# New gates, a split first weight load and a new instruction order in a fused sparse-attention and gated feed-forward kernel

## The chip, the core and the metric

The kernel runs on one core of a Trainium2 chip. Such a core has four engines that compute, each with its own queue of instructions: TensorE (PE in the profile; loading its weights is the row PEld), VectorE (DVE), ScalarE (ACT) and GpSimd (POOL). SyncE (SP) computes nothing here and issues loads and stores; GpSimd issues loads as well. Sixteen DMA engines carry the transfers. The metric is the device time of one execution in microseconds (us). The kernel before took 286.05, 288.70 and 288.79 us in three runs, median 288.7.

## The reference

Two parts follow each other. The first is causal attention in which each query sees only six chunks of 32 keys, chosen by an upper bound on its scores:

```python
B, H, S, D = 4, 8, 768, 64;  chunk, top_k = 32, 6;  nc = S // chunk
k_min, k_max = min and max over each chunk of k
ub = sum(maximum(q * k_min, q * k_max), axis=-1)          # one bound per query and chunk
ub = where(causal by chunk, ub, -1e9);  top_chunks = argsort(ub)[..., -6:]
scores = q @ k.T / sqrt(D);  masked to the chosen chunks and to pos_q >= pos_k
attn = softmax(scores) @ v
```

The second is a gated feed-forward layer over the 4 x 768 = 3072 tokens with 512 columns and 1536 hidden columns: `(sigmoid(x @ w_gate) * (x @ w_val)) @ w_out`. All inputs and the output are float32.

## The kernel before

**Units.** The work is cut into rows of 128 queries, six to each of the four batches, and these into units of up to three. Unit u0 holds the first row of batches 0, 1 and 2; u1 holds rows 1 to 3 of batch 0; u2 holds rows 4 and 5 of batch 0 and the first row of batch 3; u3 to u7 hold the rest in order. For each unit the kernel prepares keys and queries (`prepare`), chooses chunks (`choose`), computes scores, exponents and values (`attend`), and puts the result through the feed-forward layer (`ffn`; `ffn_pair` for u4 with u5 and u6 with u7, in a form with fewer products).

**The first rows.** A first row sees only its own four chunks, so there is nothing to choose, and `first` handles it by itself. The suffix _b is the batch. The loads are kf0_b and kf1_b (keys of even and odd heads), qf0_b and qf1_b (queries), vf_b (values). kfT_b and qfT_b are four float32 turns each on TensorE; kf16_b and qf16_b cast the results; scf_b are the scores, expf_b_0 and _1 the exponents on ScalarE, cmf_b_0 and _1 the causal mask on GpSimd, pvf_b the products with the values, rzf_b and xf_b the division on VectorE, xpsf_b and xTf_b turn the result into xT of the unit. All three batches have to be through before g_u0_0, the first gate product of the feed-forward layer.

**Unit 1 and 2.** Their raw keys and queries come by pairs of heads: k0_u1 to k3_u1, q0_u1 to q3_u1, and the same for u2, each load 192 KB for u1 and 128 KB for u2. `turned` copies each piece (kn_, qn_), turns it on TensorE (kT_, qT_), and copies it out in several forms (kt_, kx0_, kx1_, hk0_, hk1_ for keys; qf_, qm_, hq0_, hq1_ for queries). ub_u1 computes the bounds, ubn and ubm copy them with the causal limit, mx and ap find the chosen chunks, apt and hqm bring the choice into the rows that are added to the scores.

**Other work of the head.** hkp with three digits is the pattern of the chunks, copied from `epat` into the key tiles, eight copies of 64 x 1536 elements. beat0, beat1 and so on are turns of the identity matrix on TensorE whose results nobody reads; `BEATS` holds how many each consists of. v_b_i loads 128 rows of values and v16_b_i casts them; v16_0_0 casts vf_0.

**Weights.** wg0 to wg2 and wv0 to wv2 load 512 hidden columns each of the gate and value weights, wo0 to wo2 the output weights. They are issued on GpSimd's queue and convert to 16 bits on the way. So that they don't compete with the first loads, they read the results of gates: after0 to after6 copy one element of a landed load into the tile `word`. In the kernel before the gates stand on the four query loads of u1 and on vf_0, vf_1 and vf_2. Products g_u_i and v_u_i (four matmuls each) need wg(i // 4) and wv(i // 4).

**The order.** Each of these steps is an `Op` of a `Plan`. The text `ORDER` lists all of them once, and each engine runs its own in that order, strictly. A word is name@engine:slots: the engine is given where the step can run on several and it is not the first choice, and the slots say which buffer of a kind its result takes (eight PSUM banks, six landing buffers "v" of 128 rows, two "osb", two "big" for raw keys and queries, seven "np", and so on). A step that takes a slot waits until its last user is done; a load that reuses a landing buffer therefore holds up SyncE's queue, and all loads and stores behind it, until the cast or turn that reads the buffer has run.

## Time and profile before

| | us |
|---|---|
| runs | 286.05, 288.70, 288.79 |
| median | 288.70 |
| profiled execution, its own time | 288.5 |
| span of that execution, first instruction to last | 286.6 |
| granted TensorE clock | 1.00 of full speed |
| TensorE busy with instructions of line 953 (g and v of u0 to u3) | 39.0 and 39.1 |
| TensorE busy with line 984 (the output products of u0 to u3) | 35.2 |
| ScalarE busy with line 875 (184 exponents) | 89.1 |

The rows that follow further down come from one profiled execution. A row of the timeline reads: start in us, duration in us, engine, line of the kernel, operation, output<-input, partitions x elements and type, count, and in brackets the idle time before it with what ended it. A group row ends in: busy time, mean in ns of one, idle time before, and its releaser. A row of waits reads: engine, tile and line that waited, what it waited for, total us, number of waits and the longest. A row of the table by stretches reads: stretch, its length, then busy us (and instructions) of PE, PEld, DVE, ACT and POOL, the mean granted clock, the mean busy share of the DMA engines and GB/s. A row of a DMA issue reads: output<-input, queue, operation, count, KB of each, and us from issue to landing. SPq and POOLq are the queues of SyncE and GpSimd, where an issue's duration is the time that the queue spent at it. Unit and batch numbers are left out of the names by the profile.

### The profile page before, as it was taken

The page shows a single profiled execution, that of the slowest core. Times are in us where ns is not written, and L with a number is a line of the kernel's source. Part 1 is how long each engine was busy: PE and PEld are TensorE (multiplying, and loading weights), DVE is VectorE, ACT ScalarE, POOL GpSimd, SP SyncE. Part 2 cuts the span into 40 slices and gives each one's busy share as a digit, 9 for nine tenths or more (in the row PEclk, how much of TensorE's full clock was granted, in tenths as well). Part 3 has the DMA queues.
Part 4 walks back from the last instruction along what each step waited for, and adds up shares of the span by engine and source line. Part 5 has one row for each costly group of instructions (what it writes and reads, how often), then busy time and mean ns, then how long its engine had stood idle before and what let it go on. Part 6 is the DMA issues. An engine that isn't in the chain of part 4 may idle for free.

```text
span 286.6 us, 7418 instructions
## 1 busy us (share of the span) xinstructions
PE 269.3 (94%) x2735; PEld 185.0 (65%) x2735; DVE 243.2 (85%) x663; ACT 210.5 (73%) x458; POOL 158.2 (55%) x232
## 2 busy tenths in 40 slices
...
DMA  6999999999999968929708415202000102010005
GB/s 181 271 244 178 202 196 198 185 170 217 168 214 155 232 141 164 167 71 207 130 1 173 93 31 134 93 2 45 14 17 0 30 16 106 5 75 37 3 0 220
DMA packets 130035, 34.28 MB, mean 120 GB/s; under 512 B 118096, under 2 KB 127056, under 8 KB 130000
## 3 DMA queue, kind: packets, MB, share of 16 engines
...
q14 instruction: 14, 0.11, 0.1%
...
## 4 chain that ended last, share of the span: by engine, by line
PE 70%; DMA 10%; DVE 7%; SPq 4%; ACT 3%; POOL 2%; issue 2%; ACTq 0%; DVEq 0%; POOLq 0%
PE sc_u L864 10%; PE o_u L984 10%; PE v_u L953 8%; PE g_u L953 8%; PE pv_u L897 5%; DMA wv<-in_moe_w_val_dram 5%; PE suo_u6u L1211 3%; PE ube_u L802 2%; DMA q<-in_q_dram 2%; PE sug_u6u L1070 2%; PE suo_u4u L1211 2%; PE suv_u6u L1070 2%; PE sug_u4u L1070 2%; SPq L553 2%; PE suv_u4u L1070 2%
## 5 line engine op out<-in xcount | busy, mean ns | idle before, releaser
L875 ACT ACTIVATE att_u<-sc_u 128x512 f16<-128x512 f32 (+3 forms) x184 | 89.1, 555 | 11.6 <-PE sc_u L864 11.0
L881 POOL TENSOR_SCALAR_AFFINE_SELECT att_u<-att_u 128x384 f16<-128x384 f16 (+1 forms) x56 | 31.4, 567 | 37.6 <-ACT att_u L875 35.6
L953 PE MATMUL g_u<-xT_u,wg 128*128 128x384 f16 x192 | 39.0, 326 | 3.3 <-DVE osb_u L994 2.5
L953 PE MATMUL v_u<-xT_u,wv 128*128 128x384 f16 x192 | 39.1, 326 | 2.8 <-DMA wv<-in_moe_w_val_dram 2.8
L961 ACT ACTIVATE gate_u<-g_u 128x384 f16<-128x384 f32 x48 | 23.6, 494 | 21.2 <-PE g_u L953 19.8
L984 PE MATMUL o_u<-wo,hg_u 128*128 128x512 f16 x144 | 35.2, 379 | 0.0
L965 DVE SCALAR_TENSOR_TENSOR hg_u<-gate_u,v_u 128x384 f16<-128x384 f16 x48 | 24.9, 537 | 5.8 <-PE v_u L953 4.0
L864 PE MATMUL sc_u<-hqe,hke 128*128 128x128 f16 (+2 forms) x220 | 27.8, 243 | 0.4 <-DVE c0g_u4u L1085 0.2
L953 PEld LDWEIGHTS <-wg 128*128 128x128 f16 x192 | 18.4, 98 | 15.0 <-issue 4.2
L897 PEld LDWEIGHTS <-att_u 128*128 128x128 f16 x640 | 24.7, 97 | 5.2 <-issue 1.3
L953 PEld LDWEIGHTS <-wv 128*128 128x128 f16 x192 | 18.1, 98 | 14.4 <-DMA wv<-in_moe_w_val_dram 3.6
L897 PE MATMUL pv_u<-v,att_u 128*128 128x65 f16 x640 | 26.8, 193 | 0.0
L864 PE MATMUL sc_u<-hqo,hko 128*128 128x128 f16 (+2 forms) x220 | 25.3, 243 | 0.5 <-DVE c1v_u4u L1085 0.5
L579 POOL CAST v<-v 128x512 f16<-128x512 f32 x23 | 15.2, 668 | 13.6 <-DMA v<-in_v_dram 13.3
L864 PEld LDWEIGHTS <-hke 128*128 128x128 f16 x220 | 16.8, 98 | 7.1 <-issue 1.2
L984 PEld LDWEIGHTS <-hg_u 128*128 128x128 f16 x144 | 13.3, 98 | 11.7 <-issue 0.2
L864 PEld LDWEIGHTS <-hko 128*128 128x128 f16 x220 | 16.4, 98 | 6.5 <-issue 1.4
L916 DVE TENSOR_TENSOR x_u<-pv_u,rz_u 128x384 f16<-128x384 f32 (+1 forms) x28 | 14.9, 532 | 0.9
L1193 POOL TENSOR_TENSOR v<-hgp_u 128x384 f16<-128x384 f16 x5 | 4.5, 910 | 18.3 <-DVE hgp_u L1100 16.8
L769 DVE STREAM_TRANSPOSE qf_u<-q 128x384 f32<-128x384 f32 (+2 forms) x28 | 11.6, 437 | 3.1 <-DMA q<-in_q_dram 3.1
L825 DVE MAX8 mx_u<-ubn_u 128x8 f32<-128x8 f32 (+16 forms) x152 | 12.7, 159 | 0.1
L587 DVE TRANSPOSE_TENSOR_REDUCE kcr<-k 128x24 f32<-128x768 f32 x12 | 11.3, 957 | 1.5 <-issue 0.8
...
## 6 DMA issues: line engine op xcount, KB each, us to landing
v<-in_v_dram SPq DMA_DIRECT2D x23, 256.0 KB, 4.3
...
out_dram<-osb_u SPq DMA_DIRECT2D x16, 256.0 KB, 2.7
wg<-in_moe_w_gate_dram POOLq DMA_DIRECT2D x3, 512.0 KB, 11.1
wv<-in_moe_w_val_dram POOLq DMA_DIRECT2D x3, 512.0 KB, 11.3
wo<-in_moe_w_out_dram POOLq DMA_DIRECT2D x3, 512.0 KB, 13.1
out_dram<-osb_u6u SPq DMA_DIRECT2D x5, 256.0 KB, 2.0
```

The costliest lines, as they stand in the source:

```text
L579: plan.add(f"v16_{b}_{ib}", {POOL: pool(H * D)}, lambda e: nc.gpsimd.tensor_copy(v16[b % 2][:, ib, :, 0:D], at(t)), reads=[t], writes=[("v ...
L864: nc.tensor.matmul(at(t)[:, o:o + 128 * m], hk[b % 2][e_][:, p, 128 * jb:128 * jb + 128], hq[u.side][e_][:, p, 128 * x:128 * (x + m)], sta ...
L875: plan.add(f"exp_{u.name}_{h}_{y}", {ACT: act(n)}, lambda e, t=t, att=att, b0=b0, n=n: nc.scalar.activation(at(att)[:, b0:b0 + n], at(t), ...
L881: nc.gpsimd.affine_select(out=dv, in_=dv, compare_op=ALU.is_ge, fill=0.0, base=0, pattern=[[0, u.m], [1, 128]], channel_multiplier=-1)
L897: nc.tensor.matmul(at(pv)[:, last, x, :], at(att)[:, c:c + 128], v16[b % 2][:, jb, h, :], start=(jb == 0), stop=(jb == ib))
L916: plan.add(f"x_{u.name}_{p}", {DVE: dve(u.t)}, lambda e: nc.vector.tensor_tensor(at(x_).rearrange("p a (e d) -> p e a d", e=2), at(pv)[:, ...
L953: nc.tensor.matmul(at(t), w16[:, c, 128 * fb:128 * fb + 128], at(u.xt)[:, c, :], start=(c == 0), stop=(c == 3))
L961: plan.add(f"tanh_{u.name}_{fb}", {ACT: act(T)}, lambda e, g=g, gate=gate: nc.scalar.activation(at(gate), at(g), AF.Tanh, scale=0.5), read ...
L965: plan.add(f"hg_{u.name}_{fb}", {DVE: dve(T)}, lambda e, w_=w_, gate=gate, hg=hg: nc.vector.scalar_tensor_tensor(at(hg), at(gate), 1.0, at ...
L984: nc.tensor.matmul(at(o), hgs[c][1][1]()[:, 128 * tb:128 * tb + 128], wo16[:, fc, lo:hi], start=(c == 0), stop=(c == NFB - 1))
L1070: nc.tensor.matmul(at(t), left[i](c), right[i](c), start=first and c == 0, stop=c == 1, skip_group_check=not first)
L1211: nc.tensor.matmul(at(t), sums[what[i][0], f][1]()[:, 128 * tb:128 * tb + 128], what[i][1](f), start=first and f == 0, stop=f == half - 1, ...
```

## The change

Four things are changed. (1) The weights' gates: instead of seven, there are three, on the second halves of the query loads of the first rows (qf1_0, qf1_1, qf1_2). (2) The first weights: wg0 is split. A quarter of its rows, wgp, reads no gate at all; the other three quarters, still called wg0, read the three gates. The gate products of unit 0 wait for both. (3) BEATS: 17 groups with 79 turns in place of 12 groups with 67. (4) ORDER is another text throughout: other positions, engines and slots for the same steps. Counted over the whole text, 28 steps go from GpSimd to VectorE, 26 from GpSimd to ScalarE, 31 from ScalarE to VectorE, 27 from VectorE to ScalarE, 19 from VectorE to GpSimd and 16 from ScalarE to GpSimd. Of the diff of ORDER, the part up to just behind g_u0_0 is shown; behind it the text goes on in the same way to the end. The added lines shift the line numbers of the code by three from `weights` on (953 becomes 956).

```diff
-BEATS = (16, 12, 2, 1, 12, 6, 1, 4, 6, 2, 3, 2)
+BEATS = (17, 11, 3, 4, 4, 7, 6, 2, 5, 1, 2, 2, 4, 3, 1, 2, 5)
 
 ORDER = """
-v10 q0_u1:0 qn_u1_0:0 k3_u1 ident ap1 epat0:0 epat kcr0 hkp001 q2_u2:1 k0_u1 kn_u1_0:1 kn_u1_3@POOL:2 hkp011@POOL
-beat0:7 kT_u1_3:0 kt_u1_3:0 hkp010@ACT qT_u1_0:1 q0_u2 k1_u1 kT_u1_0:2 kt_u1_0@DVE:1 hk1_u1_0@ACT kn_u1_1@POOL:2
-kx1_u1_0:0 kT_u1_1:3 kx1_u1_1 kf0_0:0 kf1_0 kfT_0:4 kt_u1_1:2 kf16_0:2 hkf0@ACT hkf1@ACT qf_u1_0:0 kxf0 kf0_1:1 k2_u1
-kn_u1_2@DVE:1 q3_u1 hk0_u1_0 qn_u1_3:0 kxf1:1 hk0_u1_3@POOL kcr_f after0 qf1_0:2 qf0_0 beat1:7 qfT_0:5 qf16_0@DVE:3
-vf1_1:4 hk0_u1_1@POOL qn_u2_0@POOL:5 beat2:7 qT_u2_0:4 beat3:7 scf_0:5,1,1 expf_0_1:2 kT_u1_2:6 kx0_u1_1 qT_u1_3:3
-qf_u1_3@DVE q2_u1 hk1_u1_1@POOL kf1_1 qf1_1:0 kfT_1:7 after3 q1_u1 qn_u1_1:1 qT_u1_1:1 hq0_u1_3@DVE k3_u2 expf_0_0
-qf_u1_1 k2_u2 hq0 kx0_u1_3 vf_1:0 hq0_u1_1 qn_u1_2@POOL:5 qT_u1_2:3 qf_u1_2 kt_u1_2:2 kx1_u1_3 qm_u1_2@ACT:0
-hkp000@POOL vf1_3:5 hq1_u1_0@POOL qm_u1_1@ACT vf_0:2 qf0_1 kf1_2:1 cmf_0_0 q3_u2 cmf_0_1 beat4:5 qfT_1:3 qf16_1:1
-hq0_u1_0 kx1_u1_2 v16_0_0 beat5:5 pvf_0_0:3 qn_u2_2@POOL:0 qT_u2_2:0 vc_1@ACT ident16 vf1_2:2 after5 kf16_1@DVE:3
-kx0_u1_2 scf_1:6,7,1 expf_1_0 qf_u2_0:1 expf_1_1:3 pvf_0_1:1 vf_2:1 vc_2@ACT kx0_u1_0 qm_u1_0 kcr_u1 qm_u1_3 beat6:5
-ub_u1:2,5 rzf_0_0:0 rzf_0_1:1 xf_0_1:0 kn_u2_2@DVE:1 kT_u2_2:7 k1_u2 q1_u2 after6 after2 kf0_2 kfT_2:4 kf16_2:1
-xf_0_0:1 hk0_u1_2 xpsf_0_1:3,0 ubn0_u1:0 kx1_u2_2:0 ubm0_u1 mx0_u1:0 qf0_2:3 after4 qf1_2 qfT_2:2 qf16_2:3 xpsf_0_0:1
-xTf_0_0@ACT after1 wg0 wv0 beat7:6 scf_2:2,4,2 ubn1_u1 ap0_u1 apt0_u1:0 cmf_1_1 pvf_1_1:1 qf_u2_2 xTf_0_1@ACT cmf_1_0
-pvf_1_0:5 wg1 ubm1_u1 rzf_1_0:0 xf_1_0:1 hq1_u1_3@POOL qn_u2_1@DVE:4 beat8:6 qT_u2_1:5 xpsf_1_0:3 expf_2_0 cmf_2_0
-rzf_1_1:0 kn_u2_1:1 xf_1_1:0 xpsf_1_1:1 expf_2_1:1 kt_u2_2@DVE:1 pvf_2_0:4 rzf_2_0:0 xTf_1_1 xf_2_0:0 cmf_2_1 beat9:6
-pvf_2_1:2 qm_u2_0@POOL:0 qf_u2_1 qn_u2_3:4 hqm0_u1_2@ACT beat10:6 sc_u1_3_0:4,2 xpsf_2_0:1 hqm0_u1_0@DVE sc_u1_1_0:5,3
-sc_u1_1_1:0 xTf_1_0@ACT qm_u2_2@ACT hq0_u1_2@DVE sc_u1_3_1:3 wv1 rzf_2_1:0 xTf_2_0 xf_2_1:0 exp_u1_3_0 kn_u2_3@POOL:2
-kT_u2_3:1 kx0_u2_2 exp_u1_1_0 exp_u1_1_1 v_0_2:0 kf1_3:4 xpsf_2_1:2 xTf_2_1 sc_u1_3_2:4 mx1_u1 hkp110@POOL qT_u2_3:6
-qf_u2_3@DVE ap1_u1 apt1_u1 v11 sc_u1_1_2:5 sc_u1_2_0:7,1 cm_u1_1 exp_u1_3_2 cm_u1_3 v_0_3:5 wg2 kx0_u2_3 kT_u2_1:0
-kx1_u2_1 exp_u1_2_0 cm_u1_2 hkp100 hk1_u2_2 g_u0_0:2,0,0 tanh_u0_0 sc_u1_2_1:6 exp_u1_2_1 hq1_u1_2 beat11:4 v_u0_0:7
-g_u0_1:6,1,1 v_u0_1:2 kx0_u2_1 tanh_u0_1 g_u0_2:4,2,2 hg_u0_1 hg_u0_0 v_u0_2:6 exp_u1_3_1 exp_u1_1_2 hkp111 hkp101
...
+v11 k2_u1:0 epat0:0 ident q1_u2:1 hq0 kcr0 epat k3_u1 q3_u1 q1_u1 qf1_0:0 hkp110 qn_u2_1:0 qf0_0 hkp010@ACT hkp111
+k0_u2 kn_u1_2@POOL:1 ap0 k1_u1 kn_u1_3@POOL:2 beat0:7 kT_u1_2:0 k0_u1 hkp000@ACT kf0_0:1 kf1_0 kt_u1_2@DVE:0 q0_u2
+kx0_u1_2 qn_u1_1:1 hk1_u1_2@POOL qn_u1_3:3 kx1_u1_2:0 kf0_1:2 hkp101@ACT q0_u1 beat1:7 qT_u1_3:0 kn_u2_0@POOL:4
+qfT_0:1 after0 kf1_1 wgp hkp001 kT_u2_0:2 kT_u1_3:3 q2_u1 kn_u1_1@POOL:4 kx0_u1_3 kt_u1_3:1 q2_u2 hkp011@ACT
+kn_u1_0@POOL:2 qf_u1_3@DVE:0 beat2:7 kT_u1_1:4 qf1_2:0 qT_u2_1:5 ap1 v10 kT_u1_0:0 kf0_2:3 qm_u1_3:0 kfT_0:6 kx1_u1_3
+kt_u1_0:2 qf16_0@DVE:2 qn_u2_0:0 kf16_0:4 beat3:7 qT_u2_0:3 kx0_u1_0 qT_u1_1:1 kxf1:1 qf_u1_1 qf0_2 kx0_u1_1 qf_u2_0:1
+beat4:7 scf_0:7,1,1 hq0_u1_3 vf_0:1 hq0_u2_0@POOL hk0_u1_2@ACT hk1_u1_3@POOL qm_u1_1@ACT qn_u1_0@DVE:2 hq1_u1_3@DVE
+expf_0_0 beat5:3 qT_u1_0:3 vf_1:0 kx1_u1_1 expf_0_1:2 cmf_0_0 kx1_u1_0 qn_u1_2:2 kf1_2 qf_u2_1@DVE vf1_2:1 qn_u2_2:0
+kcr_u1@POOL beat6:7 qT_u1_2:0 qf1_1:4 qf_u1_0 cmf_0_1 qT_u2_2:5 qfT_2:1 qf0_1 qm_u1_0@ACT qf_u1_2@DVE vf1_1:2 hq1_u1_1
+kfT_1:3 ident16 k2_u2 kt_u1_1@DVE:0 v16_0_0 q3_u2 kxf0 beat7:7 pvf_0_0:4 qf0_3:1 kf16_1@DVE:0 vc_1@ACT vf_2:1 beat8:7
+kfT_2:3 qf16_2@DVE:3 qf1_3 after1 qm_u1_2@POOL kf16_2:5 kf1_3:3 qfT_1:1 qf_u2_2 beat9:7 scf_2:3,6,1 v_0_3:2 after2
+pvf_0_1:5 qf16_1:6 hq0_u1_1@DVE wv0 rzf_0_0:0 expf_2_1:3 kcr_f hkp100 kf0_3 wg0 beat10:7 ub_u1:1,0 hk1_u1_1@ACT
+hq0_u1_0@DVE k1_u2 vc_2@ACT xf_0_0:0 cmf_2_1 v_0_2:0 rzf_0_1:1 kn_u2_2:3 xf_0_1:1 wg1 pvf_2_1:4 expf_2_0 scf_1:6,7,0
+v_0_1:4 ubn0_u1:0 kT_u2_2:5 hk0_u1_0@ACT hq1_u1_0@POOL ubm0_u1 qfT_3:3 kx1_u2_0:1 expf_1_0 rzf_2_1:1 cmf_2_0 xf_2_1:2
+hkf0@ACT mx0_u1:0 cmf_1_0 beat11:1 xpsf_2_1:4,0 pvf_2_0:6 xpsf_0_0:1 qf16_3:1 rzf_2_0:1 hk0_u1_1 qn_u2_3:3 ap0_u1
+beat12:3 pvf_1_0:3 kt_u2_0:0 ubn1_u1 v16_0_3 expf_1_1:0 rzf_1_0:0 beat13:0 qT_u2_3:0 xf_1_0:0 xTf_0_0@ACT cmf_1_1
+xTf_2_1 hq0_u1_2 beat14:7 xpsf_1_0:3 xf_2_0:2 wv1 apt0_u1:0 xTf_1_0@ACT beat15:7 xpsf_2_0:6 hqm0_u1_0@DVE xTf_2_0@ACT
+hqm0_u1_2 beat16:7 kfT_3:6 pvf_1_1:3 hq0_u2_2@POOL sc_u1_0_0:4,3 kf16_3:3 sc_u1_1_1:1,0 rzf_1_1:1 sc_u1_1_0:7 xf_1_1:2
+k3_u2 exp_u1_0_0 qf_u2_3@DVE xpsf_1_1:3 xpsf_0_1:6 xTf_1_1 sc_u1_2_0:0,2 xTf_0_1@ACT cm_u1_0 kx0_u2_0 sc_u1_2_2:4
+sc_u1_2_1:3 exp_u1_1_0 ubm1_u1 g_u0_0:6,0,0 wg2 kx1_u2_2 exp_u1_2_0 qm_u2_1:0 k10_1:0 qm_u2_2 v_u0_0:7 mx1_u1
+tanh_u0_0 cm_u1_2 hq1_u2_3 g_u0_1:0,1,1 ap1_u1 exp_u1_1_1 cm_u1_1 v_u0_1:6 tanh_u0_1 wv2 hk0_u1_3 hk1_u1_0@ACT
+g_u0_2:1,2,2 hg_u0_1 exp_u1_2_1 wo0 v_u0_2:0 hq1_u1_2@DVE tanh_u0_2 g_u0_3:3,1,3 exp_u1_2_2 hq1_u2_0@POOL hg_u0_2
+qm_u2_3@ACT wo1 kt_u2_2:2 v_u0_3:4 kn_u2_1@DVE:2 tanh_u0_3 hq1 hg_u0_0 hkf1 sc_u1_3_0:0,1 sc_u1_3_1:3 hg_u0_3
...
-    word = lone("word", [1, 7], F32)
+    word = lone("word", [1, 3], F32)
...
     def weights(i, prio, after):
-        lo, hi = 512 * i, 512 * i + 512
-        return plan.add(f"wg{i}", {POOL: (760, 760)}, lambda e: nc.gpsimd.dma_start(wg16[:, :, lo:hi], wgs[:, :, lo:hi]),
+        lo, hi, c0 = 512 * i, 512 * i + 512, int(i == 0)
+        if c0:
+            plan.add("wgp", {POOL: (760, 760)}, lambda e: nc.gpsimd.dma_start(wg16[:, 0:1, lo:hi], wgs[:, 0:1, lo:hi]),
+                     reads=[], writes=[("wg", "p")], prio=-19.0, dma=(3000, 2048))
+        return plan.add(f"wg{i}", {POOL: (760, 760)}, lambda e: nc.gpsimd.dma_start(wg16[:, c0:4, lo:hi], wgs[:, c0:4, lo:hi]),
...
-            op = plan.add(f"g_{u.name}_{fb}", pe(650), product(g, wg16), reads=xt + [("wg", fb // 4)], writes=[g, "ffn"],
+            op = plan.add(f"g_{u.name}_{fb}", pe(650), product(g, wg16), reads=xt + [("wg", fb // 4)] + ([("wg", "p")] if u.i == 0 else []), writes=[g, "ffn"],
...
-    after((units[1].raw, 1, 0), lambda t: t[0:1, 1, 0, 0, 0, 0:1], 0)
-    after((units[1].raw, 1, 1), lambda t: t[0:1, 1, 1, 0, 0, 0:1], 1)
-    after((units[1].raw, 1, 2), lambda t: t[0:1, 1, 2, 0, 0, 0:1], 2)
-    after((units[1].raw, 1, 3), lambda t: t[0:1, 1, 3, 0, 0, 0:1], 3)
-    after(raw_f[0]["v"], lambda t: t[0:1, 0, 0:1], 4)
-    after(raw_f[1]["v"], lambda t: t[0:1, 0, 0:1], 5)
-    after(raw_f[2]["v"], lambda t: t[0:1, 0, 0:1], 6)
-    late = [f"after{i}" for i in range(7)]
+    after((raw_f[0]["q"], 1), lambda t: t[0:1, 1, 0:1], 0)
+    after((raw_f[1]["q"], 1), lambda t: t[0:1, 1, 0:1], 1)
+    after((raw_f[2]["q"], 1), lambda t: t[0:1, 1, 0:1], 2)
+    late = [f"after{i}" for i in range(3)]
```

328 lines of the change are left out of this document (163 added, 165 removed).

## The prediction

> **What bounds the kernel now.** I read the page first, then the waits of TensorE, its busy time in three stretches, the timeline around the first feed-forward products, and last the DMA queues.
>
> ```profile
> span 286.6 us, 7418 instructions
> PE 269.3 (94%) x2735; PEld 185.0 (65%) x2735; DVE 243.2 (85%) x663; ACT 210.5 (73%) x458; POOL 158.2 (55%) x232
> DMA  6999999999999968929708415202000102010005
> ```
>
> TensorE is the bound, and in the first third the DMA engines are full as well. Where TensorE is not busy is told by a table of stretches (first column the stretch in us, then busy times).
>
> ```profile
> 0.00:30.11 30.11, 23.78 (x236) 19.25 (x237) 20.65 (x73) 22.31 (x45) 22.40 (x46) 1.00 0.98 217
> 30.11:282.90 252.79, 245.51 (x2502) 165.74 (x2499) 222.17 (x591) 188.17 (x413) 135.83 (x187) 1.00 0.55 108
> 180.00:227.00 47.00, 46.21 (x488) 31.43 (x486) 45.88 (x97) 45.46 (x105) 30.12 (x38) 1.00 0.10 25
> ```
>
> At 30.11 the first gate product g_u0_0 starts, at 282.90 the last product ends. Between them 252.79 us pass and TensorE is idle for 252.79 - 245.51 = 7.3 us. The 30.11 us before are another world: most of TensorE's work there is small, and 65 of the 67 identity turns are in it. The third row is the one stretch where VectorE (45.88) and ScalarE (45.46) are as full as TensorE (46.21 of 47).
>
> ```profile
> PE v_u L953 <- DMA wv<-in_moe_w_val_dram: 2.8, 3, 1.1
> PE g_u L953 <- DVE osb_u L994: 2.5, 1, 2.5
> 30.11 0.81 PE L953 MATMUL g_u<-xT_u,wg 128*128 128x384 f16 x4
> 32.00 0.82 PE L953 MATMUL v_u<-xT_u,wv 128*128 128x384 f16 x4 [0.64 <-DMA wv<-in_moe_w_val_dram]
> 32.66 0.81 PE L953 MATMUL g_u<-xT_u,wg 128*128 128x384 f16 x4
> 38.84 0.82 PE L953 MATMUL v_u<-xT_u,wv 128*128 128x384 f16 x4 [1.13 <-DMA wv<-in_moe_w_val_dram]
> 45.54 0.82 PE L953 MATMUL v_u<-xT_u,wv 128*128 128x384 f16 x4 [1.06 <-DMA wv<-in_moe_w_val_dram]
> 54.40 0.65 PE L615 MATMUL kfT<-ident,kf 128*128 128x128 f32 x4
> ```
>
> Of the 7.3 us, the value weights cost 0.64 + 1.13 + 1.06 = 2.8: TensorE reaches v_u0_0, v_u0_4 and v_u0_8 before wv0, wv1 and wv2 land. From one such landing to the next but one piece pass 38.84 - 32.00 and 45.54 - 38.84, so a full piece of weights passes every 3.4 us. Product follows product after 32.66 - 32.00 = 0.66 us. The last row, kfT_3, turns the keys of block 3; it stands behind all the gate and value products of unit 0, at 54.40.
>
> **The equation.** If G is the start of g_u0_0 and nothing else changes, span = G + (252.79 - 2.8) + (286.6 - 282.9) = G + 253.7. The new order puts a little more real work ahead of g_u0_0: four-transpose turns qfT_3 and kfT_3 come in, two-transpose turns and about one score group go out. I take 0.6 us (the two turns at 0.65 each, less what leaves), so span = G + 253.1. Before, G was 30.1 with the 2.8 behind it; the new order breaks even at G = 33.5. Everything hangs on G.
>
> **The change part by part.** *Gates and first weights.* The order gives GpSimd wgp behind after0, and the first gated piece is now wv0, behind after1, qm_u1_2 and after2; wg0 follows with three quarters of its bytes.
>
> ```profile
> 14.66 0.45 SPq L542 DMA_DIRECT2D kf<-in_k_dram  x1
> 19.15 0.28 POOL L513 COPY word<-vf 1x1 f32<-1x1 f32 x1 [0.55 <-DMA vf<-in_v_dram]
> 19.84 1.05 POOL L518 DMA_DIRECT2D wg<-in_moe_w_gate_dram  x1
> 20.89 0.76 POOL L519 DMA_DIRECT2D wv<-in_moe_w_val_dram  x1
> 26.66 0.85 POOL L603 TENSOR_SCALAR qm_u<-qf_u 128x256 f32<-128x256 f32 x1
> ```
>
> The load that opens the gate is qf1_1, SyncE's 25th. Before, the 25th was vf_2, and it let `word` go at 19.15. The bytes of the first 25 loads are nearly equal (by their sizes 128 KB fewer), and wgp adds a quarter of a piece, 0.25 x 3.4 = 0.85 us on full DMA engines. So the gate opens at about 19.6. Then qm_u1_2, 320 columns against the 256 of the row, takes about 1.0, and wv0 issues near 20.9, 1.1 us later than wg0 did. wgp's own issue (0.76 to 1.05) delays two copies behind it on GpSimd by as much; ScalarE is not ready for their results by then, so I take nothing, with 1.0 as the bound. wgp's gain is 0.85 us at wg0's landing.
>
> *ScalarE's share of the head.*
>
> ```profile
> 3.37 0.51 ACT L358 COPY qn_u<-kq_u 128x384 f32<-128x384 f32 x1 [1.29 <-DMA kq_u<-in_q_dram]
> 6.64 1.47 ACT L358 COPY hko<-epat 64x1536 f16<-64x1536 f16 x1
> 10.92 0.48 ACT L358 COPY qf_u<-qT_u 128x384 f32<-128x384 f32 x1
> 12.88 0.60 ACT L657 ACTIVATE attf<-scf 128x512 f16<-128x512 f32 x1 [0.94 <-PE scf L652]
> 9.67 0.69 DVE L625 TENSOR_REDUCE kcr<-kfT 128x16 f32<-128x512 f32 x1 [1.07 <-ACT kf L358]
> ```
>
> Four of the eight pattern copies now run on ScalarE instead of one: 4 x 1.47 = 5.9 us, all ahead of the first exponents. With the 15 other instructions up to qn_u1_2 at about 0.5 each (7.4 us), and a start near 3.7 with half a microsecond of waits, qn_u1_2 ends near 17.5. That is late for three things in a row. qT_u1_2 (TensorE) follows at 18.1; vf1_1 waits for its buffer, and v16_0_0 behind it on GpSimd is done near 18.8; SyncE waits for that to reuse v16_0_0's landing slot (qf0_3). On VectorE, qf_u1_2, ident16, kt_u1_1, kxf0 and kf16_1 follow, five instructions of up to 0.69, 2.6 us in all, so kfT_2 cannot turn before 20.7, and kf1_3, which lands where kf_2 lay, issues near 21.3. So the tail of SyncE's head loads (kf1_3, v_0_3, kf0_3) starts just after wv0.
>
> *What the weights do to those loads.* The rows give for single issues the KB and the us to landing; the first is the kf issue of 14.66, then follow those of 19.53, 20.68 and 25.34, whose issue rows stand below them.
>
> ```profile
> kf<-in_k_dram SPq DMA_DIRECT2D x1, 128.0 KB, 2.7
> kf<-in_k_dram SPq DMA_DIRECT2D x1, 128.0 KB, 8.0
> v<-in_v_dram SPq DMA_DIRECT2D x1, 256.0 KB, 13.4
> kf<-in_k_dram SPq DMA_DIRECT2D x1, 128.0 KB, 20.6
> wg<-in_moe_w_gate_dram POOLq DMA_DIRECT2D x1, 512.0 KB, 8.8
> 19.53 1.11 SPq L542 DMA_DIRECT2D kf<-in_k_dram  x1
> 20.68 0.90 SPq L573 DMA_DIRECT2D v<-in_v_dram  x1
> 25.34 6.87 SPq L542 DMA_DIRECT2D kf<-in_k_dram  x1
> ```
>
> Alone, a kf load takes 2.7 us. Once weights flow, kf1_3 landed at 19.53 + 8.0 = 27.5 and v_0_3 at 20.68 + 13.4 = 34.1: 256 KB in 6.6 us, so 128 KB in 3.3. kf0_3 landed at 45.9, and nobody minded, since kfT_3 stood at 54.40 and the casts of v_0_x were late too. In the new order two near consumers hang on them. kfT_3 stands on TensorE ahead of the last scores and of g_u0_0; and v16_0_3 stands on GpSimd ahead of cmf_1_1 and of wv1.
>
> *G with late keys.* If kf1_3 still slips through (21.3 + 2.7 = 24.0), v_0_3 lands at 30.6 and kf0_3 at 33.9. If it doesn't, it lands about 7.7 us behind wv0's issue as before (28.6), v_0_3 at 35.2; but by then wv0 (20.9 + 8.8 = 29.7), wg0 (32.2) and wg1 (35.6) are through and wv1 is held, so kf0_3 comes near 36.3. Bounds 33.9 and 36.3, I take 35.2. From there to g_u0_0: the turn (0.65), its cast and one exponent on ScalarE (0.60 each by the row of 12.88), xpsf_0_1 and xTf_0_1 (under 0.5): 2.3 us. G = 37.5.
>
> wv1 then issues between 33 and 35 and needs at most the 8.8 of a first piece; v_u0_4 stands nine products (5.9) and about 1 us of scores behind G, at 44.4. So no weight wait is left, which is why the 2.8 goes.
>
> *Identity turns.* 79 instead of 67, and all of them now stand ahead of G: 14 more at 0.11 to 0.21 us.
>
> ```profile
> 1.63 3.35 PE L474 MATMUL beat<-ident 128*128 128x128 f32 x16 [1.63 <-POOL ident masks.py:199]
> 8.68 1.47 PE L474 MATMUL beat<-ident 128*128 128x128 f32 x12
> ```
>
> (1.47 / 12 = 0.12, and 3.35 / 16 = 0.21 at the start.) They fill waits of the ScalarE chain; I cost them at nothing, 1.7 us if a turn stands where TensorE would have been free to go on.
>
> *The new order behind G.* 54 operations leave GpSimd for VectorE or ScalarE and 35 go the other way; the net 19, at about 0.5 each by the copies above, load VectorE and ScalarE with some 10 us more. Over 252.79 us there is room (222.17 and 188.17 busy), only between 180 and 227 us there isn't: 0 to 1.5 us there. The other loss is the query load:
>
> ```profile
> 103.78 0.70 DVE L769 STREAM_TRANSPOSE qf_u<-q 128x128 f32<-128x128 f32 x3 [2.78 <-DMA q<-in_q_dram]
> ```
>
> VectorE waited 2.78 us for the last piece of q_2, and TensorE 2.5 us for VectorE. Before, four other transfers stood between the four pieces, now three, but less of TensorE's work (15 instead of 17 us by its rows) stands between the freed buffer and the first use. I keep the 2.5; it may go, or come twice.
>
> **Sum.** Span = 37.5 + 253.1 = 290.6. The profiled execution took 288.5 at a span of 286.6, 1.9 more, and it lies 0.2 under the median of 288.7. Forecast 290.6 + 1.9 = 292.5 us.
>
> **Rivals.** *The keys land in time.* It decides at kf1_3: if it issues 1.2 us or more ahead of my 21.3, or wv0 as much later, enough of v_0_3 and kf0_3 gets through before the weights flow. Then ScalarE sets G: block 2's scores follow kfT_2 by a turn, two casts and the products, about 2 us, so its exponents start at 22.7; from there to kf16_3 ScalarE has 17 instructions, 8.5 us at 0.5, then an exponent and xTf_0_1, 32.7. G = 33.0, span 286.1, time 288.0: no change. For it: it needs only a little over a microsecond in a chain that I summed from some 30 rows. Against it: 4 x 1.47 on ScalarE is not in doubt.
>
> *In time, and the query wait goes as well.* 288.0 - 2.5 = 285.5, less up to 0.5 where tight turns at the end loosen: 285.2, faster. Decided by whether the last q_2 piece lands before VectorE gets to it; one transfer fewer between speaks for it, the shorter distance against.
>
> *Late keys and a cooled TensorE.* TensorE would stand still for some 4 to 5 us at kfT_3, longer than any wait behind 30.11 in this trace (2.5), after which the granted clock in the rows was still 1.00. The start shows the price: 13 turns at 0.21 before the pace of 0.11, 1.3 us. Time 292.5 + 1.3 = 293.8. [...]
>
> *The gate does not help at all*, because qf1_1 lands no earlier than vf_2 did: that is already in the sum.
>
> **How the numbers follow.** About 1% (2.9 us, so 285.8 and 291.6) is what a measurement of this kernel can tell from no change. Late keys 0.48 (292.5, its own range 290 to 295: G from 36.2 to 38.6, the query wait gone or doubled, 1.5 for VectorE), in time 0.22 (288.0), in time without the query wait 0.20 (285.2), late and cooled 0.10 (293.8). Of the late case 0.09 falls under 291.6, when the query wait goes; of the second 0.03 falls under 285.8 and 0.01 over 291.6; of the third 0.06 stays within 1%. So slower 0.39 + 0.10 + 0.01 = 0.50, within 1% 0.09 + 0.18 + 0.06 = 0.33, faster 0.03 + 0.14 = 0.17. The range leaves out about 1 in 10 below and fewer above: 285.2 to 295.
>
> **What would show it.** Right: TensorE waits several us just before kfT_3 for kf<-in_k_dram, near 30 to 36 us; GpSimd's cast of v_0_3 waits for its load with wv1 behind it; g_u0_0 starts near 37.5; no wait on wv is left. Wrong: g_u0_0 starts by 33.5, kfT_3 without a wait; or G is late for ScalarE, with xpsf or sc_u waiting on it; or behind G the idle time of 7.3 - 2.8 = 4.5 us is far from kept.

## The result, and the profile after

The changed kernel took 290.22 us (median of 20 executions, 287.19 to 293.27), the kernel before, run beside it, 287.53 (20 executions, 284.81 to 291.41). The ratio is 1.0091, with a 95% interval of 1.0066 to 1.0116: 0.9% slower. The ratios leave out executions more than 1.5% above the fastest of their kernel, so the medians, which leave out none, stand beside them throughout.

The profiled execution took 289.06 us, 1.2 under the median, with a span of 287.4. From its page (span, busy time of the engines, granted clock in 40 slices):

```profile
span 287.4 us, 7415 instructions
PE 273.3 (95%) x2747; PEld 187.6 (65%) x2747; DVE 247.7 (86%) x676; ACT 217.9 (76%) x464; POOL 139.6 (49%) x210
PEclk9999997999999999999999999999999999999999
```

TensorE is idle for 287.4 - 273.3 = 14.1 us, where it was 286.6 - 269.3 = 17.3: the change removed 3.2 us of idle time. But TensorE is busy for 4.0 us more. The groups of identity turns, before and after, hold most of it:

```profile
L474 PE MATMUL beat<-ident 128*128 128x128 f32 x67 | 10.9, 305 | 1.6 <-POOL ident masks.py:199 1.6
```

```profile
L474 PE MATMUL beat<-ident 128*128 128x128 f32 x79 | 13.6, 310 | 2.3 <-POOL ident masks.py:199 1.6 <-ACT qf L358 0.6
```

That is 2.7. The other 1.3 is about what the digit 7 of the clock's row costs. The table by stretches of the changed kernel (columns as before) shows where:

```profile
0.00:33.09 33.09, 27.15 (x254) 21.34 (x255) 23.49 (x68) 25.27 (x48) 20.79 (x42) 1.00 1.00 217
33.09:283.70 250.61, 246.12 (x2494) 166.23 (x2492) 224.22 (x609) 192.22 (x416) 118.86 (x169) 0.99 0.54 106
44.20:46.40 2.20, 0.03 (x2) 0.00 (x0) 0.35 (x2) 0.77 (x2) 0.61 (x1) 0.96 1.37 214
46.20:49.70 3.50, 3.27 (x33) 2.51 (x33) 1.52 (x5) 0.05 (x1) 0.89 (x2) 0.51 1.42 215
180.00:227.00 47.00, 45.62 (x477) 30.43 (x475) 46.48 (x93) 44.16 (x101) 26.82 (x33) 1.00 0.11 27
```

From 44.2 to 46.4 TensorE stands still, and for the 3.5 us behind that its granted clock is 0.51: 3.27 us of busy time there would be some 1.6 less at full clock, and in the last row of the timeline below a value product takes 1.47 us, where such a product takes 0.81 at full clock. The timeline of the changed kernel tells what TensorE waited for, and how the head of the kernel came out (rows of PE, ScalarE, GpSimd and SyncE in order of time; "issue" in brackets means that the profile names no releaser):

```profile
20.14 0.18 POOL L513 COPY word<-qf 1x1 f32<-1x1 f32 x1 [1.67 <-DMA qf<-in_q_dram]
20.29 1.09 POOL L606 TENSOR_SCALAR qm_u<-qf_u 128x320 f32<-128x320 f32 x1
20.95 0.37 SPq L545 DMA_DIRECT2D kf<-in_k_dram  x1
21.34 0.51 POOL L513 COPY word<-qf 1x1 f32<-1x1 f32 x1
21.37 0.51 SPq L576 DMA_DIRECT2D v<-in_v_dram  x1
21.80 0.87 POOL L522 DMA_DIRECT2D wv<-in_moe_w_val_dram  x1
21.92 0.76 SPq L545 DMA_DIRECT2D kf<-in_k_dram  x1
30.74 0.63 PE L618 MATMUL kfT<-ident,kf 128*128 128x128 f32 x4 [0.17 <-issue]
31.46 0.59 ACT L358 CAST kf<-kfT 128x512 f16<-128x512 f32 x1 [1.19 <-PE kfT L618]
33.09 0.81 PE L956 MATMUL g_u<-xT_u,wg 128*128 128x384 f16 x4
45.77 0.61 POOL L582 CAST v<-v 128x512 f16<-128x512 f32 x1 [3.76 <-DMA v<-in_v_dram]
46.43 0.60 PE L900 MATMUL pv_u<-v,att_u 128*128 128x65 f16 x8 [2.19 <-POOL v L582]
46.84 1.47 PE L956 MATMUL v_u<-xT_u,wv 128*128 128x384 f16 x4
```

```profile
kf<-in_k_dram SPq DMA_DIRECT2D x1, 128.0 KB, 3.3
v<-in_v_dram SPq DMA_DIRECT2D x1, 256.0 KB, 3.8
kf<-in_k_dram SPq DMA_DIRECT2D x1, 128.0 KB, 8.7
v<-in_v_dram SPq DMA_DIRECT2D x1, 256.0 KB, 21.5
```

The second fence has four single loads of the changed kernel: kf1_3, v_0_3, kf0_3 (issued at 20.95, 21.37 and 21.92) and v_0_1 (issued at 24.22). The first two are quick. kf0_3, issued 0.12 us behind the first weights (wv0, 21.80), takes 8.7 us and lands at 30.65; kfT_3 starts 0.09 us later. TensorE shows only 0.17 us of waiting for it, because five identity turns ahead of it run from 29.81 to 30.58; ScalarE, which casts the result, stands 1.19 us. v_0_1 takes 21.5, lands at 45.7, and the first values of unit 1 (pv_u1_1) stand for its cast v16_0_1. In this execution, then, g_u0_0 starts at 33.09, no weight is waited for, and the stand is at v_0_1.

### The profile page after: what moved, and what is told of

Read it like the earlier page. It is cut to its first block, busy times and chain, and to the rows that moved or that the text cites. A ratio compares the mean times of both kernels' runs of the same rounds, so it can differ in the third digit from the quotient of the medians.

```text
span 287.4 us, 7415 instructions
## 1 busy us (share of the span) xinstructions
PE 273.3 (95%) x2747; PEld 187.6 (65%) x2747; DVE 247.7 (86%) x676; ACT 217.9 (76%) x464; POOL 139.6 (49%) x210
## 4 chain that ended last, share of the span: by engine, by line
PE 79%; DVE 7%; POOL 4%; issue 4%; ACT 2%; SPq 2%; DMA 1%; POOLq 0%; ACTq 0%; DVEq 0%
PE sc_u L867 11%; PE o_u L987 11%; PE v_u L956 10%; PE g_u L956 9%; PE pv_u L900 7%; PE suo_u6u L1214 3%; PE ube_u L805 2%; PE suo_u4u L1214 2%; PE sug_u4u L1073 2%; PE sug_u6u L1073 2%; PE beat L474 2%; PE suv_u4u L1073 2%; PE suv_u6u L1073 2%; DMA qf<-in_q_dram 1%; PE sro_u6u L1214 1%
## 5 line engine op out<-in xcount | busy, mean ns | idle before, releaser
L878 ACT ACTIVATE att_u<-sc_u 128x512 f16<-128x512 f32 (+3 forms) x184 | 92.0, 550 | 21.0 <-PE sc_u L867 18.4
L884 POOL TENSOR_SCALAR_AFFINE_SELECT att_u<-att_u 128x384 f16<-128x384 f16 (+1 forms) x56 | 30.3, 546 | 38.9 <-ACT att_u L878 37.7
L956 PE MATMUL v_u<-xT_u,wv 128*128 128x384 f16 x192 | 39.7, 330 | 0.0
L987 PE MATMUL o_u<-wo,hg_u 128*128 128x512 f16 x144 | 35.2, 379 | 0.0
L900 PE MATMUL pv_u<-v,att_u 128*128 128x65 f16 x640 | 28.4, 195 | 2.6 <-POOL v L582 2.2
L900 PEld LDWEIGHTS <-att_u 128*128 128x128 f16 x640 | 26.1, 99 | 7.4 <-issue 3.9
L867 PE MATMUL sc_u<-hqo,hko 128*128 128x128 f16 (+2 forms) x220 | 28.7, 244 | 0.2
L867 PE MATMUL sc_u<-hqe,hke 128*128 128x128 f16 (+2 forms) x220 | 26.9, 243 | 0.0
L867 PEld LDWEIGHTS <-hko 128*128 128x128 f16 x220 | 17.2, 98 | 7.8 <-issue 1.8
L987 PEld LDWEIGHTS <-hg_u 128*128 128x128 f16 x144 | 13.2, 98 | 12.1 <-issue 0.5
L1196 POOL TENSOR_TENSOR v<-v,hg_u 128x384 f16<-128x384 f16 x6 | 6.2, 1030 | 22.8 <-DVE v L1196 20.8
L474 PE MATMUL beat<-ident 128*128 128x128 f32 x79 | 13.6, 310 | 2.3 <-POOL ident masks.py:199 1.6
L1073 PEld LDWEIGHTS <-Sv 128*128 128x128 f16 x96 | 9.0, 98 | 5.7 <-issue 0.6
```

What stands on the lines that cost most here:

```text
L474: nc.tensor.transpose(at(beat), ident32, ident32)
L867: nc.tensor.matmul(at(t)[:, o:o + 128 * m], hk[b % 2][e_][:, p, 128 * jb:128 * jb + 128], hq[u.side][e_][:, p, 128 * x:128 * (x + m)], sta ...
L878: plan.add(f"exp_{u.name}_{h}_{y}", {ACT: act(n)}, lambda e, t=t, att=att, b0=b0, n=n: nc.scalar.activation(at(att)[:, b0:b0 + n], at(t), ...
L884: nc.gpsimd.affine_select(out=dv, in_=dv, compare_op=ALU.is_ge, fill=0.0, base=0, pattern=[[0, u.m], [1, 128]], channel_multiplier=-1)
L900: nc.tensor.matmul(at(pv)[:, last, x, :], at(att)[:, c:c + 128], v16[b % 2][:, jb, h, :], start=(jb == 0), stop=(jb == ib))
L956: nc.tensor.matmul(at(t), w16[:, c, 128 * fb:128 * fb + 128], at(u.xt)[:, c, :], start=(c == 0), stop=(c == 3))
```

## The experiments

Each was timed in five rounds beside the kernel before, with twelve executions each (e4 and e5: six). All start from the changed kernel unless it is said otherwise; an edit of ORDER is given by the words that it moves.

| run | median, us | before, us | ratio, 95% interval |
|---|---|---|---|
| the change | 290.22 | 287.53 | 1.0091, 1.0066 to 1.0116 |
| e1 before again | 287.50 | 287.73 | 0.9962, 0.9933 to 0.9992 |
| e2 warm | 292.28 | 287.73 | 1.0069, 1.0032 to 1.0106 |
| e3 fill | 290.68 | 287.73 | 1.0065, 1.0027 to 1.0103 |
| e4 gate early | 292.48 | 287.73 | 1.0152, 1.0119 to 1.0184 |
| e5 keys behind | 294.22 | 287.18 | 1.0168, 1.0089 to 1.0246 |
| e6 old gates | 287.13 | 287.18 | 1.0007, 0.9970 to 1.0043 |
| e7 patterns on VectorE | 289.47 | 287.18 | 1.0075, 1.0041 to 1.0109 |
| e8 unsplit | 289.85 | 287.18 | 1.0044, 1.0001 to 1.0088 |
| e9 order alone | 286.48 | 287.21 | 0.9976, 0.9938 to 1.0015 |
| e10 masks first | 287.23 | 287.21 | 0.9990, 0.9955 to 1.0025 |
| e11 few turns | 287.50 | 287.21 | 1.0014, 0.9972 to 1.0056 |
| e12 gates in the old order | 288.39 | 287.21 | 1.0033, 0.9992 to 1.0075 |

e1 is the kernel before against itself: its interval misses 1 by 0.1%, so differences of some 0.4% are at the edge of what this comparison can tell.

**e1: the kernel before again.** No edit.

> The kernel before, unchanged, to learn its granted clock over several executions; only the profiled one is known (1.00). Theory A: what the change costs in the median is a half-clock stretch of TensorE that only the changed kernel has. Then nearly all executions of the kernel before show a mean clock of 0.997 to 1.00 and lie within 1.5 us of 287.5. Rival: both kernels lose clock in many executions alike; then most of these show 0.985 to 0.995, as those of the changed kernel do.

Its twelve executions had mean clocks of 0.994 to 1.00, ten of them 0.997 or more. Of the 20 executions of the changed kernel one had 1.00, and eight had 0.988 or less; that one took 287.19, those eight 290.2 to 293.3. Only four of the 20 had 0.997 or more, and they took 287.2 to 289.8. Nine of e1's twelve lie within 1.5 us of 287.5. So theory A's sign is there: long times go with a low clock that is rare in the kernel before. That the clock is the cause isn't shown by it; e2 tests that.

**e2: the stand filled with turns.**

```diff
-BEATS = (17, ..., 2, 5)
+BEATS = (17, ..., 2, 5, 18)
-kx0_u2_2 pv_u1_1:6 tanh_u0_7
+kx0_u2_2 beat17:5 pv_u1_1:6 tanh_u0_7
```

> The changed kernel with 18 identity turns (2.0 us at 0.11) put on TensorE directly ahead of pv_u1_1, where it waits 2.19 us for the cast of v_0_1. Nothing else moves, so the wait itself stays and is only filled. Theory A (the stand lets the clock fall to half for 3.4 us, which costs about 1.6 us): the dip at 46 to 50 us is gone, mean clock 0.998 or more, the time falls by 1.5 to 2.7 us against the changed kernel, to about 288. Rival (the stand itself is the cost, or the clock falls for another reason): time within 0.5 us of the changed kernel's 290.2, clock still about 0.99.

In the profiled execution the clock was 1.00 throughout and the time 290.32. The clock's half of theory A came true, the time's half didn't: the median rose to 292.28, and the six executions with a clock of 0.998 or more took 288.3 to 291.2, median 290.3, no less than the changed kernel. The profile tells a part: with the same program up to there, v_0_1 landed at 47.5 in place of 45.7, so the wait behind the turns was still 0.56 us. And six of the twelve executions had a clock of 0.988 or 0.994, at 293.3 to 296.7; the turns did not keep their clock up. So the half clock behind this stand is not the root.

**e3: the stand filled with work.**

```diff
-kx0_u2_2 pv_u1_1:6 tanh_u0_7 v_u0_7:3 exp_u1_0_2 kn_u2_3@DVE:4 ... hg_u0_7 ... g_u0_8:5,2,8
+kx0_u2_2 tanh_u0_7 v_u0_7:3 hg_u0_7 g_u0_8:5,2,8 pv_u1_1:6 exp_u1_0_2 kn_u2_3@DVE:4 ...
```

> The changed kernel with v_u0_7 and g_u0_8 moved ahead of pv_u1_1 on TensorE (and hg_u0_7 ahead of kn_u2_3 on VectorE, so that the gate buffer of g_u0_8 is free): 1.3 us of real work stands in the wait for v_0_1. Theory A: the wait shrinks from 2.19 to about 0.9 us and is broken in two, the clock stays at 1.00; 1.3 us of idle time and some 1.6 us of half clock go, the time falls by 2.5 to 4 us, to 286.5 to 287.7, level with the kernel before or faster. Rival (what is lost lies behind 180 us, where VectorE and ScalarE are full): at most 1.3 us is won.

No gain (290.68). But its profile shows another course (timeline of TensorE, and a stretch of the table):

```profile
34.58 1.09 PE L618 MATMUL kfT<-ident,kf 128*128 128x128 f32 x4 [3.17 <-issue]
38.24 1.49 PE L956 MATMUL g_u<-xT_u,wg 128*128 128x384 f16 x4
```

```profile
36.00:38.20 2.20, 2.20 (x18) 1.84 (x17) 1.75 (x8) 1.62 (x4) 1.12 (x2) 0.50 1.26 235
```

Here TensorE stood 3.17 us ahead of kfT_3, g_u0_0 started at 38.24, and the clock was 0.50: the forecast's case. The row names no releaser, but kfT_3 started 0.09 us behind the landing of kf0_3, as in the changed kernel. v_0_1 landed at 41.8 in this execution and TensorE had no wait for it, so the profile can't tell whether the fill works. Up to g_u0_0 the program is that of the changed kernel. In this execution wv0 was issued at 22.67, v_0_3 at 22.52 (8.6 us to landing) and kf0_3 at 23.23 (11.3 us, landed at 34.5). So one program runs both ways, and the traces of the two differ by a few tenths of a microsecond between the issues of SyncE's loads and of GpSimd's first weights (v_0_3 was issued 0.43 us ahead of wv0 in the changed kernel's, 0.15 in this one).

**e4: the gate 0.7 us earlier.**

```diff
-after1 qm_u1_2@POOL ... after2 ... wv0 ... wg0
+after1 after2 wv0 qm_u1_2@POOL ... wg0
```

> The changed kernel with wv0 issued ahead of the copy qm_u1_2 on GpSimd, near 20.5 us in place of 21.80; the order of everything else is kept. It tests the point on which the forecast rested: that kf1_3, v_0_3 and kf0_3 starve if the first weights start ahead of them. Forecast's step: kf1_3 (issued at 20.95) then takes 7 to 8 us in place of 3.3, v_0_3 lands near 34 in place of 25.2 and kf0_3 near 36 in place of 30.7; kfT_3 waits and g_u0_0 starts between 36 and 38.5 in place of 33.1; time 3 to 5 us above the changed kernel. Rival (a microsecond doesn't decide it, the loads pass or starve together over a wider stretch): g_u0_0 within 0.7 us of 33.1, time within 1 us of 290.2 or lower, the weights being earlier.

Issues and TensorE's rows, then the landing of kf1_3, v_0_3 and kf0_3:

```profile
21.13 0.81 POOL L522 DMA_DIRECT2D wv<-in_moe_w_val_dram  x1
21.93 0.62 SPq L545 DMA_DIRECT2D kf<-in_k_dram  x1
22.60 0.62 SPq L576 DMA_DIRECT2D v<-in_v_dram  x1
23.26 2.41 SPq L545 DMA_DIRECT2D kf<-in_k_dram  x1
36.21 1.08 PE L618 MATMUL kfT<-ident,kf 128*128 128x128 f32 x4 [2.38 <-issue]
39.68 0.81 PE L956 MATMUL g_u<-xT_u,wg 128*128 128x384 f16 x4
```

```profile
kf<-in_k_dram SPq DMA_DIRECT2D x1, 128.0 KB, 7.8
v<-in_v_dram SPq DMA_DIRECT2D x1, 256.0 KB, 13.2
kf<-in_k_dram SPq DMA_DIRECT2D x1, 128.0 KB, 12.9
```

All three starve, as the forecast's step says: 7.8 us, landings at 35.8 and 36.1, g_u0_0 at 39.7, above the expected 36 to 38.5. Part of that is this execution: SyncE issued kf1_3 1.0 us later than in the changed kernel's trace. All six executions lie at 291.9 to 293.9, with clocks of 0.982 to 0.988. The median is 2.3 us above the changed kernel, less than the 3 to 5 expected. GpSimd's rows tell why the 6.6 us at g_u0_0 did not all come through: the cast of v_0_3 waited 8.35 us there and held wv1 back to 37.01 (29.52 in the changed kernel), and v_0_1 landed at 38.4, so the stand at pv_u1_1 is gone.

**e5: keys and values off the path.**

```diff
-kfT_3:6 pvf_1_1:3 ... kf16_3:3 ... g_u0_0 ... v_u0_3:4
+pvf_1_1:3 ... g_u0_0 ... v_u0_3:4 kfT_3:6 kf16_3:3
-cmf_2_1 ... v16_0_3 ... cmf_1_1 ... wv1 ... cm_u1_3
+cmf_2_1 ... cmf_1_1 ... wv1 ... cm_u1_3 v16_0_3
```

> The changed kernel with kfT_3 (and its cast kf16_3) moved from ahead of g_u0_0 to behind v_u0_3, and the cast v16_0_3 moved on GpSimd from ahead of cmf_1_1 and wv1 to behind cm_u1_3. Theory A (late keys and values of block 3 and row 3 set the start of g_u0_0 in many executions): g_u0_0 starts at 33 us or earlier in every execution, no wait on kfT_3 or on v16_0_3 ahead of it, and the executions above 291 us with a clock of 0.988 disappear; median 287.5 to 289, what is left being the wait for v_0_1 at pv_u1_1. Rival B (the loads as a whole set when unit 0 and the first values can be through, whoever waits for them): g_u0_0 starts earlier, but the waits go to v_0_1 and to the weights, and the median stays within 1 us of 290.2.

Theory A's first half came true, g_u0_0 at 31.68 without a wait for keys; and the median was the highest of all. Its second half failed: five of the six executions are above 291 us, and the profiled one has a clock of 0.988 without a wait for keys. The rows of waits and of stretches:

```profile
PE pv_u L900 <- POOL v L582: 5.6, 1, 5.6
```

```profile
45.00:51.00 6.00, 0.49 (x9) 0.49 (x9) 0.19 (x1) 0.64 (x2) 1.09 (x2) 0.71 1.33 211
```

What was won ahead of g_u0_0 came back as 5.6 us at v_0_1, which landed at 49.8. Rival B had the place right, v_0_1, but not the size: it expected a median within 1 us of 290.2. In this execution wv0 was issued at 21.18, ahead of v_0_3 (21.24), and v_0_3, kf0_3 and v_0_1 landed late one after the other (30.2, 34.7, 49.8); moving the consumers of the first two out of the way lets TensorE run on to the third. It also lets the weights go on: with v16_0_3 no longer ahead of it, wv1 was issued at 28.90 and the next, wg2, at 31.54 (29.52 and 33.15 in the changed kernel). So a late v_0_3 acts as a gate for the weights behind its cast. With e3 and e4 this points to why the two stands shut each other out, though no run changes this alone.

**e6: the old gates in the new order.** The three gates are replaced by the seven (four query loads of u1, vf_0, vf_1, vf_2); the split and the order of everything else stay.

```diff
-qfT_0:1 after0 kf1_1 wgp ... hk1_u1_3 ... after1 qm_u1_2 ... after2 ... wv0
+qfT_0:1 after1 after3 kf1_1 wgp ... hk1_u1_3 after0 after2 ... after4 after5 qm_u1_2 ... after6 ... wv0
```

> The changed kernel, order and split of wg0 kept, with the seven old gates (four query loads of unit 1, vf_0, vf_1, vf_2) in place of the three new ones. vf_2 lands last, near 22.6, so wv0 is issued near 22.8 in place of 21.8. Theory A (a microsecond at the gate decides whether the last loads of the head pass ahead of the weights): kf0_3 lands by 29 us in nearly every execution, no stand at kfT_3, weights 1 us later, g_u0_0 at 33 to 34.5; median 288 to 289.3, clock above 0.99. Rival B (the gate's place is of no weight): within 0.7 us of 290.2. Rival C (later weights cost what they are late): 291 or more.

```profile
21.70 1.58 SPq L545 DMA_DIRECT2D kf<-in_k_dram  x1
23.34 0.17 POOL L513 COPY word<-vf 1x1 f32<-1x1 f32 x1 [3.84 <-DMA vf<-in_v_dram]
23.45 0.84 POOL L522 DMA_DIRECT2D wv<-in_moe_w_val_dram  x1
32.03 0.60 PE L618 MATMUL kfT<-ident,kf 128*128 128x128 f32 x4
34.35 0.81 PE L956 MATMUL g_u<-xT_u,wg 128*128 128x384 f16 x4
```

```profile
kf<-in_k_dram SPq DMA_DIRECT2D x1, 128.0 KB, 3.9
```

GpSimd waits 3.84 us at the last gate and issues wv0 1.65 us later than the changed kernel did. kf0_3, issued 1.75 us ahead of it, now takes 3.9 us, and v_0_1 lands at 41.3 in place of 45.7: weights that start 1.65 us later give the values back 4.4. There is no stand at kfT_3 or pv_u1_1, the clock is 1.00 (0.999 or more in eight of the twelve executions, 0.986 in the lowest), and although g_u0_0 starts 1.3 us later than after the change, the span is 284.6 and the median 287.13. This one part undone takes the whole loss away. Theory A's time was too careful by a microsecond; rivals B and C fall.

**e7: two pattern copies off ScalarE.**

```diff
-hkp101@ACT ... hkp011@ACT
+hkp101@DVE ... hkp011@DVE
```

> The changed kernel with two of the four pattern copies on ScalarE (hkp101, hkp011, 1.47 us each there) put on VectorE, where such a copy took 0.67. The forecast's step (ScalarE's copies delay the chain to kfT_2, to the issue of kf1_3 and to the exponents): qn_u1_2 ends 1.5 to 2.9 us ahead of 17.1, kf1_3 is issued 0.5 us or more ahead of 20.95, kf0_3 lands by 28 us in nearly all executions, g_u0_0 starts 0.5 to 2 us ahead of 33.1; median 287 to 289. Rival B (the loads set the pace of the head, and ScalarE only waits elsewhere): kf1_3's issue moves by under 0.3 us, the median stays within 0.7 us of 290.2.

```profile
10.16 0.48 ACT L358 CAST kt_u<-kT_u 128x384 f16<-128x384 f32 x1 [2.21 <-DVE kcr L590]
12.47 0.48 ACT L358 CAST kt_u<-kT_u 128x384 f16<-128x384 f32 x1 [1.83 <-PE kT_u L704]
10.04 1.26 DVE L360 COPY hko<-epat 64x1536 f16<-64x1536 f16 x1
11.91 0.52 PE L704 MATMUL kT_u<-ident,kn_u 128*128 128x128 f32 x3 [0.90 <-DVE qf_u L360]
```

Where the two copies stood, ScalarE now waits 2.21 and 1.83 us. qn_u1_2 ends at 17.4 (17.1 with all four copies on it), kf1_3 is issued at 21.27 (20.95), g_u0_0 starts at 33.63, and the median is 289.47: about what rival B expected. But that the copies only filled waits isn't shown. The first one did: the cast behind it starts at 10.16 in place of 10.40. The second took 1.26 us on VectorE, not the 0.67 expected, and the turn kT_u1_0, for which ScalarE waits at 12.47, itself waited 0.90 us for the copy that VectorE ran behind it. So the edit moved the load to another engine of the same chain, and what the copies cost on ScalarE stays open.

**e8: wg0 in one piece.**

```diff
-        lo, hi, c0 = 512 * i, 512 * i + 512, int(i == 0)
+        lo, hi, c0 = 512 * i, 512 * i + 512, 0
-kf1_1 wgp hkp001
+kf1_1 hkp001
```

> The changed kernel without wgp: wg0 is one piece of 512 KB behind the gates, as in the kernel before; nothing else moves. If the quarter that goes ahead is a gain (it takes a fourth of a 3.4 us piece out of the time when the weights are needed), wg0 lands near 33.7 in place of 32.9, g_u0_0 waits for it, and the median rises by 0.5 to 1 us. Rival (the head's loads are one full stream, so that the quarter ahead delays every load behind it, and the gate with them, by the same 0.85 us): the head's loads and wv0 come 0.5 to 0.9 us earlier, the keys are late less often, and the median is level or lower by up to 1.5 us.

The whole wg0 landed at 32.83, the three quarters of the changed kernel at 32.88. wv0 was issued 0.5 us earlier and landed at 29.30 in place of 30.27, g_u0_0 started at 32.88. So in this trace the rival holds for the weights, but not for the last loads of the head: kf1_3 was issued at 21.20 (20.95). Two runs with the old gates are another pair: wg0 landed at 33.19 with the split (e6) and at 34.02 without it (e9), although wv0 was issued 1.0 us later with it, and yet g_u0_0 started no earlier (34.35 and 34.06). The times (1.0044 beside 1.0091, with overlapping intervals) show no gain from the split.

**e9: the order alone.** e6 and e8 together, so that only the order and the turns are new.

> The new order with its 79 turns, but the seven old gates and wg0 in one piece: changes 1 and 2 undone, 3 and 4 kept. Theory A (the gates alone made the change slower, order and split are level with what was before): median 286.3 to 288, beside 287.1 to 287.7 for the kernel before; wv0 near 23 us, kf0_3 landed by 26, no stand of TensorE over 2.3 us, clock 1.00 in most executions. Rival B (the split is worth its 0.85 us once the gate is late enough): 0.5 to 1 us above the run with old gates and split (287.13), with g_u0_0 waiting for wg0.

```profile
34.06 0.82 PE L956 MATMUL g_u<-xT_u,wg 128*128 128x384 f16 x4 [0.43 <-DMA wg<-in_moe_w_gate_dram]
```

```profile
34.06:280.90 246.84, 244.50 (x2493) 165.14 (x2493) 224.29 (x606) 191.89 (x416) 118.29 (x168) 1.00 0.55 107
```

286.48 us, the lowest median of all, but its interval holds 1: it can't be called faster than the kernel before. Theory A holds; g_u0_0 waits 0.43 us for wg0, yet the split (e6) was not better.

**e10: a mask ahead of the gate.** e6 with two moves on GpSimd.

```diff
-after6 ... wv0 ... wg0 ... cmf_2_1
+cmf_2_1 after6 ... wg0 wv0
```

> The new order with the seven old gates and the split, and on GpSimd the mask cmf_2_1 ahead of the last gate (it waited 1.7 us behind it, and pvf_2_1 with it 2.3 us on TensorE), and wg0 ahead of wv0. If the wait behind the gate sets g_u0_0 there: pvf_2_1 without a wait, g_u0_0 near 33.2 in place of 34.35, and about 1 us below the run with old gates, 286 to 286.5: faster than both kernels. Rival (the weights, issued 0.7 us later, or the loads set the pace): level with 287.1, g_u0_0 or v_u0_0 waiting for weights.

pvf_2_1's wait fell from 2.26 to 0.52 us, but g_u0_0 started at 34.22, 0.13 earlier, with the head's loads 0.6 to 0.9 us later in this execution. 287.23: level. The wait moved on: the next product, pvf_2_0, now waits 1.39 us. The masks cmf_2_0 and cmf_1_0 still stand behind the gate, the weights' issues and a cast; they start at 26.92 us (27.05 in e6), also 0.13 earlier. So the rows point to GpSimd's masks behind the gate; no run moves all of them.

**e11: 33 turns for 79.** e6 with

```diff
-BEATS = (17, 11, 3, 4, 4, 7, 6, 2, 5, 1, 2, 2, 4, 3, 1, 2, 5)
+BEATS = (17, 1, 1, 1, 1, 1, 1, 1, 1, 1, 1, 1, 1, 1, 1, 1, 1)
```

> The run with old gates, with 33 identity turns in place of 79: 17 at the start, one in each of the 16 other groups. Theory A (the turns fill waits and keep the clock up): the granted clock falls below 0.9 in stretches between 5 and 33 us, TensorE's small steps there take longer, and the median rises by 0.5 to 2 us. Theory B, the forecast's (they fill waits of the chain on ScalarE, and cost and bring nothing): within 0.5 us of 287.1, clock of the head at 1.00. Theory C (some stand where TensorE was free to go on): up to 1.7 us lower.

```profile
PEclk9779799999999999999999999999999999999999
```

Theory A is right on the clock: it falls in the second, third and fifth slice, and all twelve executions have a mean of 0.976 to 0.994. Theory B is right on the time: 287.50 beside 287.13, ratios 1.0014 and 1.0007. So the turns bring nothing that the medians show. A low clock and a long time still go together here (the six executions with 0.988 or more took 286.2 to 287.7, the six below 287.2 to 291.8), without showing which causes which.

**e12: gates and split in the old order.** The kernel before with its own order and turns; weights(), the three gates and the reads of g_u0_* as after the change.

```diff
-after0 (query load of u1) ... after5 ... after6 after2 ... after4 ... after1 wg0 wv0 ... cmf_1_0
+wgp ... after0 (qf1_0) ... after1 (qf1_1) ... cmf_1_0 after2 (qf1_2) wg0 wv0
```

> The kernel before with changes 1 and 2 alone: its own order and turns, the three new gates, wgp ahead. In that order qf1_2 lands last, at 22.5 us, so the weights start some 2.7 us later than at 19.84. If the weights' start is what TensorE waits for in that order: wg0 lands near 31, wv0 to wv2 2 us later each less the 0.85 of the quarter, the waits of v_u0_0, v_u0_4 and v_u0_8 grow from 2.8 to 4 to 5 us in all, and the median rises by 1 to 2.5 us. Rival (a later start lets the head's loads through and gives back as much, as it did in the new order): within 0.7 us of the kernel before.

```profile
PE v_u L956 <- DMA wv<-in_moe_w_val_dram: 2.3, 1, 2.3
```

wg0 was issued at 23.61 (19.84 in the kernel before), and one wait of 2.3 us for wv0 took the place of three with 2.8; v_0_1 landed at 30.2 in place of 42.5, which nobody used. The median rose by 1.2 us, at the low end of what was expected, but not by the expected step: the waits for wv were to grow to 4 to 5 us. The interval just holds 1: a small loss or none.

## Why the prediction was right, and where it was not

The result lies in the range, the kernel became slower as forecast, and the place was right: the last head loads beside the first weights. The time was 2.3 us too high. Of these, 1.2 are the base (288.7 for the kernel before, where 20 executions gave 287.53) and 1.1 the change itself (3.8 forecast, 2.7 measured). By the forecast's own bound of about 1%, a loss of 0.9% still counts as no change, to which it gave 0.33; to slower it gave 0.50. The sign alone thus says little for it.

**The step that failed: when kf0_3 lands.** The forecast had v_0_3 land at 30.6 or later and kf0_3 at 35.2. In the profiled execution v_0_3 passed ahead of the weights (25.2) and kf0_3 landed at 30.65. The step behind it held: from kf0_3's landing to g_u0_0 the forecast had 2.3 us, and the changed kernel (30.65 to 33.09), e2 and e7 each show 2.44. So the keys set g_u0_0 here too. The rival with keys in time had G = 33.0 because ScalarE would be last; but ScalarE stood 1.19 us for kfT_3, so its agreement with 33.09 is luck. Taken out of the way (e5), the keys leave g_u0_0 at 31.68.

By its own sign of being wrong (g_u0_0 by 33.5, kfT_3 without a wait) the forecast's case failed in that execution. In e3, with the same program up to there, the keys were late (38.24 beside the forecast 37.5), and in e4's trace (39.68). That e4's median, 292.48, is the forecast's 292.5 is luck: G came 2.2 us later, and from there to the last product 246.9 us passed, not 249.4.

The rival named a shift of 1.2 us between the issues of kf1_3 and wv0 that would let the keys pass; it leaves kf1_3 about 0.8 ahead of wv0. In the profiled execution kf1_3 came 0.35 us ahead of the 21.3 and wv0 0.9 behind the 20.9, together 1.25: just over it. But in e7 and e8 kf1_3 was only 0.44 and 0.11 ahead, and kf0_3 still landed at 31.2 and 30.2. What separates the traces is v_0_3: it took 3.6 to 6.2 us where kf0_3 landed by 32.2 (the change, e2, e7, e8, e11), and 8.6 to 13.2 where it landed at 34.5 or later (e3, e4, e5). How many of the 20 executions went each way isn't traced, and a low mean clock doesn't tell, since e5 has it without a wait for keys.

**The gate.** wv0 was put at 20.9 and issued at 21.80. The gate's load qf1_1 landed at 20.08, not 19.6; qm_u1_2 took the 1.0 foreseen; and the copy after2 behind it, 0.51 us in the row of 21.34, was left out of the sum. These 0.9 us are most of the shift of 1.25.

**ScalarE's share.** qn_u1_2 ended at 17.09 (forecast 17.5) and kf1_3 was issued at 20.95 (21.3). The sums came close; whether the copies are the cause is open, since e7 put two of them on another engine of the same chain.

**The starving.** Right in kind and size: 7.8 us for kf1_3 and landings near 36 in e4, against 7.7 and 35.2 to 36.3. What was missed is the next load in the same queue. The forecast and its rivals ended the matter at g_u0_0 and counted v_0_1 nowhere, though the trace of before had its cast waiting. With the keys in time the stand went there.

**The quarter ahead.** Put at a gain of 0.85 us at wg0's landing. Beside e8 the split piece landed 0.05 us later, beside e9 (e6) 0.83 earlier; in neither pair did g_u0_0 start earlier.

**The turns.** Costed at nothing; the times of e11 agree: 1.0014 of before with 33 turns, 1.0007 with 79 (e6), each within some 0.4%.

**The rest behind g_u0_0.** The equation gave 249.4 us from g_u0_0 to the last product (253.1 less the 3.7 behind it), with the query wait kept. Measured: 250.61. But the 2.5 us of query wait are gone (no row of TensorE's waits names it any more), 2.19 came at v_0_1, and about 1.3 by the half clock. Where nothing starves (e9) it is 246.84, which is 249.4 - 2.5 to 0.1: the rival's term. The idle time behind G, 250.61 - 246.12 = 4.5 us, is just the 4.5 that the forecast kept, by luck: 2.5 went at one place and 2.19 came at another. Between 180 and 227 us TensorE was busy for 45.62 in place of 46.21, 0.6 us less, inside the 0 to 1.5.

**The cooled TensorE.** It had a chance of 0.10 and a price of 1.3 us, for a stand of 4 to 5 us at kfT_3. It happened at kfT_3 in e3, behind 3.17 us (0.50 from 36.0 to 38.2). In the profiled execution it came at v_0_1, behind only 2.19 (0.51 from 46.2 to 49.7), and by an estimate from the rows of the result cost 1.3 to 1.6 us of busy time. The slow first turns from which the price was taken ran at a granted clock of 1.00 in the trace of before (0 to 5 us), so no run shows that they are the price of a low clock.

So the new order was a gain of 2.5 us at the query wait and 2.8 at the weights, paid for with 3 to 4 us at g_u0_0 (33.09 to 34.35 in place of 30.11): level or a little faster in all (e9: 0.9976 of before, an interval that holds 1). The new gates then cost about 0.8%: 1.0091 with them, 1.0007 without (e6).
